# Routed attention and a tanh-shrink MLP on one core: the order of value products, narrow sum products, and some earlier steps

## The chip, the cores and the metric

The kernel runs on one core of a Trainium2 chip. The metric is the device time of one execution in microseconds (us), median of several runs. A difference of about 0.2% can be told from no change.

## The reference, cut to what matters

```python
# q, k, v: (4, 8, 768, 64); centroids: (8, 16, 64); w_in: (512, 2048); w_out: (2048, 512)
q_assign = argmax(q_n @ c_n.T)          # the nearest of 16 centroids, for each query
k_assign = argmax(k_n @ c_n.T)          # and for each key
scores = where(q_assign == k_assign, q @ k.T / 8, -1e9)
attn = softmax(scores)                  # over the 768 keys
x = (attn @ v), heads side by side      # (3072, 512)
h = x @ w_in
out = (h - tanh(h)) @ w_out             # (3072, 512)
```

All arithmetic is float32 in effect. The two weight matrices come in as 64-bit floats and are rounded on the chip.

## The kernel before, in words

**Order of the work.** The order on every engine is written out by hand: the builder runs through a Python loop over 96 `steps` (L856, L983) and each engine carries out its instructions in the order in which they were issued. Nothing is rescheduled later. A pair `n` is one batch element and two heads, so there are 16 pairs, four for each of the four batch elements; a pair has two halves of 384 queries, and each half has three steps of 256 keys. The first twelve steps are the first halves of pairs 0 to 3, the next twelve their second halves; from pair 4 on a pair's halves follow each other.

**A step.** `begin` (L411) computes the scores `sc` of the *following* step on TensorE and the exponential on ScalarE; `select` (L443) multiplies by the routing mask on VectorE: it compares a `row` of query codes with a key code (L451). `value` (L466) then multiplies the resulting weights `e` with the values into `av` (L473). In the first halves of pairs 1 to 3 (`masked`) the mask comes instead from a small extra product with one-hot codes `hot` (L430). The row sums that softmax divides by are products with a matrix of ones: for the first halves of pairs 0 to 3 (`summed`, L350) they are taken on TensorE in every step, four products of 64 columns (L482), of which two fit beside each other in the array; elsewhere GpSimd adds the weights up (L460, L464) and one product follows (L501). `take` (L489) copies `av` to `xT`; `total` (L494) copies the sums to `den`. For pairs that are not `soon` (L517; `soon` are pairs 2, 3, 7, 11 and 15) the sums travel through DRAM to be inverted: `list` (L511), `compact` (L520, back as `each`), `invert` (L526), `spread_out` (L532), `scale` (L539), one per step. The others are divided on the spot (`divide`, L543), and GpSimd adds their sums up in `wholes` (L507).

**Getting a pair ready** (`before`, L860) runs steps ahead in numbered stages: 0 `turns` transposes q and k on TensorE (`pt`, L300), ScalarE copies them out (`t`, L307), and the next loads are issued on SP; 1 `similar` (L313) multiplies with the centroids, four products of 32 columns that fit beside each other (`sim`, L319), copied by ScalarE (L324); 2 `route` (L326) transposes (`pr`, L332) and finds the codes on VectorE (L338 to L345); 3 `publish` (L359) writes the codes to DRAM (L364, L368, L370); for pairs 1 to 3 also 4 `spread_both` (L382: `hot`, read back over all partitions) and 5 `one_hot` (L390). In the loop, stage 1 comes first in its step (L1003), then `begin` (L1007), then `value` (L1013). Stage 0 is called between the pieces of other TensorE work (L1061); where a step has none, that is after the values and sums.

**The weights.** `fetch` (L185, GpSimd's queue) loads one of 32 pieces of 512 KB into one of three `raw` buffers, `rest_of` (L195) takes its low words on ScalarE (L140) and `round_piece` (L200) its high words on VectorE (L145 to L152) and fetches the piece after the next two. How many pieces belong to a step is written in `paces` (L980).

**The MLP** of batch element 0 is done plainly (L557) between the steps 12 to 47. Those of elements 1 to 3 use seven products of quarters instead of eight (`strassen_items`, L722): eight times seven `up_product` (`pu`, L761), then seven times three `down_product` (`pd`, L809). `right_factors` (L711) forms differences of `xT` on VectorE first; four of the seven up products need them, of the others the first two in order (`PRODUCTS`, L617: 1, 2, 6, 7, 4, 5, 3) do not. `up_product` puts the quarters of h together in `G` on VectorE (L747), and `shrink` (L749) subtracts the tanh: ScalarE takes the tanh of a tile of 768 columns (L751) and GpSimd subtracts it (L752). `fetch_factors` (L678) loads the factors of the item after the next into one of three `stream` buffers over SP's queue. The last element's items (L1072 to L1105) come after the loop; a check of all inputs and sums on VectorE (L1077 to L1098) stands after the first two of them.

PSUM holds two double tiles for scores and transposes, one tile for `av`, and three tiles for everything else (L164 to L166).

Of the kernel before, what the change touches and what calls it, by code (L numbers as in the profile page):

```python
# [30 lines left out]
F32 = mybir.dt.float32  # L31
# [3 lines left out]
ALU = mybir.AluOpType  # L35
ACT = mybir.ActivationFunctionType
AX = mybir.AxisListType

P = 128
# [18 lines left out]
def kernel(  # L58
# [43 lines left out]
    smallest = const.tile([P, 2 * len_pieces], F32, name="smallest")  # L102
    largest = const.tile([P, 4 * (HP - 1)], F32, name="largest")
    each = const.tile([P, 2 * (B * (HP - 1) - 1), 2 * TB // P], F32, name="each")
    flag = const.tile([1, 1], I32, name="flag")

    out_r = out.rearrange("(b p j) m -> b j p m", p=P, j=NCH)
# [46 lines left out]
    def fast():  # L154
# [195 lines left out]
        def summed(n: int, half: int):  # L350

            return n < HP and half == 0
# [113 lines left out]
        def value(n: int, half: int, s: int):  # L466
            e = weights.pop((n, half, s))
            if s == 0:
                avs[n, half] = ps_a.tile([P, TB], F32, name="av", tag="a")
            for i in range(2):  # L470
                j = 2 * s + i
                for h in range(2):
                    nc.tensor.matmul(  # L473
                        avs[n, half][h * D : h * D + D], lhsT=vals[n][:, h, j], rhs=e[i][:, h],
                        start=(j == 0), stop=(j == NCH - 1),
                    )
            if summed(n, half):
                if s == 0:
                    sums[n, half] = ps_f.tile([P, TB], F32, name="den", tag="f")
                for i in range(2):  # L480
                    for h in range(2):
                        nc.tensor.matmul(  # L482
                            sums[n, half][h * D : h * D + D], lhsT=ones, rhs=e[i][:, h],
                            start=(s + i == 0), stop=(2 * s + i == NCH - 1),
                        )

        dens = {}

# [5 lines left out]
        def total(n: int, half: int):  # L494

            s = sums.pop((n, half))
            ps = s
            if not summed(n, half):
                ps = ps_f.tile([P, TB], F32, name="den", tag="f")
                for h in range(2):  # L500
                    nc.tensor.matmul(  # L501
                        ps[h * D : h * D + D], lhsT=ones, rhs=s[:, h], start=True, stop=True
                    )
            t = dens[n, half] = sump.tile([P, TB], F32, name="den")
            nc.scalar.activation(out=t, in_=ps, func=ACT.Copy, bias=EPS)
            if soon(n):
                nc.gpsimd.tensor_tensor(out=wholes, in0=wholes, in1=t, op=ALU.add)  # L507
                return
            lists[n, half] = dram.tile([2, TB], F32, name="list")
            for h in range(2):  # L510
                nc.sync.dma_start(lists[n, half][h : h + 1], t[h * D : h * D + 1])  # L511

# [4 lines left out]
        def soon(n: int):  # L517
            return pairs[n][1] == HP - 1 or n == HP - 2

        def compact(n: int, half: int):  # L520
            spots[n, half] = each[:, len(spots)]
            nc.sync.dma_start(
                spots[n, half], lists.pop((n, half)).rearrange("h n -> (h n)").rearrange("(p i) -> p i", p=P)
            )

        def invert(n: int, half: int):  # L526
            t = spots[n, half]
            nc.vector.reciprocal(out=t, in_=t)
            back = lists[n, half] = dram.tile([2, TB], F32, name="back")
            nc.sync.dma_start(back.rearrange("h n -> (h n)").rearrange("(p i) -> p i", p=P), t)  # L530
# [177 lines left out]
            late_pools["G"] = late_pools["g"].tile([P, HF, 2, 2, TB], F32, name="G")  # L708
            late_pools["S1"] = late_pools["left"].tile([P, HF, TB], F32, name="S1")

        def right_factors(b: int):  # L711

            d = diffs[b] = late_pools["diff"].tile([P, 3, CH, TB], F32, name="diff")
            for c in range(CH):
                x, y = xT[b * HP + c], xT[b * HP + CH + c]
                for out, u, w in (
                    (d[:, 0, c], x[:, 1], x[:, 0]), (d[:, 1, c], y[:, 1], d[:, 0, c]),
                    (x[:, 1], y[:, 1], x[:, 1]), (d[:, 2, c], y[:, 0], d[:, 1, c]),
                ):
                    nc.vector.tensor_tensor(out=out, in0=u, in1=w, op=ALU.subtract)  # L720

        def strassen_items(b: int):  # L722
            base = (b - 1) * PER
# [4 lines left out]
            def up_product(i: int, k_: int, between):  # L728
                which = PRODUCTS[k_]
                x = [xT[b * HP + c] for c in range(CD)]  # L730
                d = diffs[b]
                right = {
                    1: [x[c][:, 0] for c in range(CH)], 2: [x[CH + c][:, 0] for c in range(CH)],
                    3: [x[CH + c][:, 1] for c in range(CH)], 4: [d[:, 2, c] for c in range(CH)],
                    5: [d[:, 0, c] for c in range(CH)], 6: [d[:, 1, c] for c in range(CH)],
                    7: [x[c][:, 1] for c in range(CH)],
                }[which]
                if k_ == 0:
                    held[i] = (
                        late_pools["s"].tile([P, TB], F32, name="s"),  # L740
                        late_pools["u"].tile([P, 2, TB], F32, name="u"),
                    )
                s, u = held[i]
                g = G[:, i]

                def add(out, x, y):
                    nc.vector.tensor_tensor(out=out, in0=x, in1=y, op=ALU.add)  # L747

                def shrink(f: int):  # L749
                    th = late_pools["th"].tile([P, 2, TB], F32, name="th")  # L750
                    nc.scalar.activation(out=th, in_=g[:, f], func=ACT.Tanh)  # L751
                    nc.gpsimd.tensor_tensor(  # L752
                        out=g[:, f].rearrange("p a n -> p (a n)"),
                        in0=g[:, f].rearrange("p a n -> p (a n)"),
                        in1=th.rearrange("p a n -> p (a n)"), op=ALU.subtract,
                    )

                ps = ps_f.tile([P, TB], F32, name="pu", tag="f")
                for c in range(CH):
                    for r in halves:  # L760
                        nc.tensor.matmul(  # L761
                            ps[r], lhsT=streams[base + i][:, c, k_, r], rhs=right[c],
                            start=(c == 0), stop=(c == CH - 1),
                        )
                if which == 1:
                    nc.scalar.copy(out=s, in_=ps)
                    fetch_factors(base + i + 2)
                elif which == 2:
                    add(g[:, 0, 0], ps, s)
                elif which == 6:  # L770
                    add(u[:, 0], ps, s)
                elif which == 7:
                    add(u[:, 1], ps, u[:, 0])
                elif which == 4:
                    add(g[:, 1, 0], ps, u[:, 1])
                elif which == 5:
                    add(u[:, 0], ps, u[:, 0])
                    add(g[:, 1, 1], ps, u[:, 1])
                    shrink(1)
                else:  # L780
                    add(g[:, 0, 1], ps, u[:, 0])
                    shrink(0)
                between()
                if k_ == len(PRODUCTS) - 1:

                    nc.gpsimd.tensor_tensor(out=left1[:, i], in0=g[:, 0, 1], in1=g[:, 1, 1], op=ALU.add)
                    nc.gpsimd.tensor_tensor(
                        out=g[:, 0, 1], in0=g[:, 0, 0], in1=g[:, 0, 1], op=ALU.subtract
                    )
                    streams.pop(base + i)  # L790
# [283 lines left out]
        for it in tail[:2]:  # L1074
            it[2](lambda: None)

# [213 lines left out]
```

## Time and profile before

| | us |
|---|---|
| median of three runs | 1012.71 (1012.15 to 1013.81) |
| the profiled execution, its own time | 1012.54 |
| its span, first to last instruction | 1010.8 |
| TensorE busy (PE) | 987.7 |
| VectorE busy (DVE) | 551.7 |
| GpSimd busy (POOL) | 502.8 |
| ScalarE busy (ACT) | 298.8 |

In views of the profile, PE is the matmul side of TensorE and PEld its weight loader, SP the engine that issues most transfers. A timeline line gives the start, the time from the first start to the last end of the merged instructions, engine, line, operation, output and inputs, the array's shape (rows*columns), the operand's shape and how many records were merged; in brackets the idle time before it and what ended it. A float32 matmul leaves two records and a transpose one. Records overlap, since matmuls are pipelined; how long a group holds TensorE is read from its start to the start of the next.

### The profile page before, as it was taken

To read this page: it belongs to the slowest core of one execution; us is meant where nothing else is said; L and a number is where in the kernel's file an instruction comes from. 1 tells how busy PE (TensorE), PEld (TensorE's weight loads), DVE (VectorE), ACT (ScalarE), POOL (GpSimd) and SP (SyncE) were. 2 spreads that over 40 slices of the span, in tenths; PEclk is the share of its full clock that TensorE was granted. 3 is DMA by queue.
4 is the path that set the end of the run, shared out by engine and by line. 5 is a ranking of instruction groups with operands and counts; after the bars stand their busy time and mean duration, and the time that the engine had idled before them with its cause. 6 is when DMAs were issued, how large, how long until landed. Compare 5 with 4: busy or idle time off the path is not lost.

```text
span 1010.8 us, 16557 instructions
## 1 busy us (share of the span) xinstructions
PE 987.7 (98%) x6444; PEld 470.6 (47%) x6444; DVE 551.7 (55%) x1047; ACT 298.8 (30%) x458; POOL 502.8 (50%) x343
## 2 busy tenths in 40 slices
PE   8989999999999999999999999999999999999997
PEld 4433443344443334444455555444445555444665
DVE  6457887737666566747544357655645336543011
ACT  4434443233432323332331222324331221122000
POOL 1014344545354554865777244675679345465600
PEclk9999999999999999999999999999999999999999
DMA  7653434214564823453445637344443232233221
GB/s 218 174 135 114 134 125 127 72 51 125 134 176 139 261 90 123 135 169 110 173 123 178 189 128 216 108 147 119 146 162 92 98 108 81 92 110 122 104 95 40
DMA packets 115681, 132.46 MB, mean 131 GB/s; under 512 B 62688, under 2 KB 95372, under 8 KB 112908
## 3 DMA queue, kind: packets, MB, share of 16 engines
q1 hardware_dynamic: 109212, 109.80, 35.7%
q0 software_dynamic: 6240, 21.50, 6.2%
q8 instruction: 53, 0.87, 0.4%
q14 instruction: 32, 0.26, 0.1%
q10 hardware_dynamic: 144, 0.03, 0.0%
HBM read 110.14 MB, written 21.17 MB: 130 GB/s over the span
## 4 chain that ended last, share of the span: by engine, by line
PE 91%; DVE 3%; DMA 1%; ACT 1%; POOL 1%; issue 1%; SPq 0%; DVEq 0%; ACTq 0%; POOLq 0%
PE pd L809 20%; PE pu L761 20%; PE sc L419 13%; PE av L473 13%; PE o L584 8%; PE h L568 8%; PE sim L319 2%; PE den L501 2%; PE pt L300 2%; PE den L482 1%; PE warm L270 1%; ACT t L307 1%; POOL G L752 1%; PE pr L332 1%; DMA hot<-q_codes 1%
## 5 line engine op out<-in xcount | busy, mean ns | idle before, releaser
L464 POOL TENSOR_TENSOR sum<-sum,e 128x768 f32<-128x768 f32 x112 | 207.3, 1850 | 106.5 <-DVE e L451 102.8
L451 DVE SCALAR_TENSOR_TENSOR e<-row,code,sc 128x384 f32<-128x384 bf16 x336 | 185.5, 608 | 94.7 <-ACT sc L441 78.6
L809 PE MATMUL pd<-stream,G 128*64 128x256 f32 x1728 | 192.4, 379 | 2.4 <-POOL G L752 2.4
L441 ACT ACTIVATE sc<-sc 128x768 f32<-128x768 f32 x168 | 126.2, 792 | 209.5 <-PE sc L419 207.4
L809 PEld LDWEIGHTS pd<-stream,G 128*64 128x64 f32 x1728 | 123.5, 137 | 70.5 <-issue 8.0
L473 PE MATMUL av<-e,vals 128*64 128x384 f32 x768 | 147.0, 502 | 4.7 <-ACT xT L492 3.8
L419 PE MATMUL sc<-t,t 64*128 64x384 f32 x768 | 149.9, 509 | 0.3 <-ACT e L441 0.3
L752 POOL TENSOR_TENSOR G<-G,th 128x768 f32<-128x768 f32 x48 | 87.4, 1833 | 104.6 <-ACT th L751 104.6
L761 PE MATMUL pu<-xT,stream 128*64 128x384 f32 x768 | 134.6, 487 | 0.7 <-DVE top L340 0.7
L761 PE MATMUL pu<-diff,stream 128*64 128x384 f32 x576 | 103.5, 488 | 1.9 <-DVE u L747 1.5
L419 PEld LDWEIGHTS sc<-t,t 64*128 64x128 f32 x768 | 66.0, 186 | 73.6 <-issue 41.6
L460 POOL TENSOR_TENSOR sum<-e 128x768 f32<-128x768 f32 x28 | 58.0, 2071 | 70.9 <-DVE e L451 62.6
L473 PEld LDWEIGHTS av<-e,vals 128*64 128x64 f32 x768 | 47.1, 136 | 89.6 <-issue 83.2
L761 PEld LDWEIGHTS pu<-xT,stream 128*64 128x64 f32 x768 | 54.6, 137 | 68.5 <-issue 61.5
L568 PE MATMUL h<-xT,w_in 128*64 128x384 f32 x512 | 86.2, 486 | 0.1
L584 PE MATMUL o<-w_out,g 128*64 128x512 f32 x384 | 86.1, 593 | 0.0
L751 ACT ACTIVATE th<-G 128x768 f32<-128x768 f32 x48 | 40.3, 843 | 123.0 <-DVE G L747 119.4
L761 PEld LDWEIGHTS pu<-diff,stream 128*64 128x64 f32 x576 | 40.5, 137 | 52.5 <-issue 44.3
L747 DVE TENSOR_TENSOR G<-pu,u 128x384 f32<-128x384 f32 x72 | 39.8, 553 | 40.8 <-PE pu L761 40.5
L568 PEld LDWEIGHTS h<-xT,w_in 128*64 128x64 f32 x512 | 36.6, 137 | 46.0 <-issue 44.7
L584 PEld LDWEIGHTS o<-w_out,g 128*64 128x64 f32 x384 | 27.3, 137 | 49.8 <-issue 49.3
L820 DVE TENSOR_TENSOR c<-pd,du 128x256 f32<-128x256 f32 x36 | 15.1, 420 | 62.8 <-PE pd L809 62.8
(121 smaller groups left out, 850.2 us busy)
## 6 DMA issues: line engine op xcount, KB each, us to landing
stream<-up_factors SPq DMA_DIRECT2D x24, 896.0 KB
stream<-down_factors SPq DMA_DIRECT2D x21, 1024.0 KB
raw<-in_moe_w_in_dram POOLq DMA_DIRECT2D x16, 512.0 KB, 5.3
raw<-in_moe_w_out_dram POOLq DMA_DIRECT2D x16, 512.0 KB, 4.4
again<-in_moe_w_in_dram SPq DMA_DIRECT2D x32, 256.0 KB
again<-in_moe_w_out_dram SPq DMA_DIRECT2D x32, 256.0 KB
x<-in_q_dram SPq DMA_DIRECT2D x32, 192.0 KB
x<-in_k_dram SPq DMA_DIRECT2D x32, 192.0 KB
```

The source lines that it names most:

```text
L419: nc.tensor.matmul(sc[i][:, h, 0:TB], lhsT=turned[n, 1][r].rearrange("p a n -> p (a n)")[:, j * P : (j + 1) * P], rhs=turned[n, 0][r, half ...
L441: nc.scalar.activation(out=out, in_=sc[i][:, :, 0:TB], func=ACT.Exp, scale=SCALE)
L451: nc.vector.scalar_tensor_tensor(out=e[:, h], in0=rows[n, half][:, h], scalar=codes[n][:, 1, j // HCH, h, j % HCH : j % HCH + 1], in1=sc[: ...
L460: nc.gpsimd.tensor_tensor(out=s, in0=pair[0], in1=pair[1], op=ALU.add)
L464: nc.gpsimd.tensor_tensor(out=s, in0=s, in1=pair[i], op=ALU.add)
L473: nc.tensor.matmul(avs[n, half][h * D : h * D + D], lhsT=vals[n][:, h, j], rhs=e[i][:, h], start=(j == 0), stop=(j == NCH - 1),)
L568: nc.tensor.matmul(h[r], lhsT=w_in[i][:, c, o * P : (o + 1) * P][:, r], rhs=xT[c][:, half], start=(c == 0), stop=(c == CD - 1),)
L584: nc.tensor.matmul(acc[sub][r], lhsT=gs[f % HF][:, f // HF, sub * P : (sub + 1) * P][:, r], rhs=w_out[f // FQ][:, f % FQ], start=(f == seq ...
L751: nc.scalar.activation(out=th, in_=g[:, f], func=ACT.Tanh)
L752: nc.gpsimd.tensor_tensor(out=g[:, f].rearrange("p a n -> p (a n)"), in0=g[:, f].rearrange("p a n -> p (a n)"), in1=th.rearrange("p a n -> ...
L761: nc.tensor.matmul(ps[r], lhsT=streams[base + i][:, c, k_, r], rhs=right[c], start=(c == 0), stop=(c == CH - 1),)
L809: nc.tensor.matmul(ps[r], lhsT=left(i)[:, r], rhs=t[:, i], start=(i == 0), stop=(i == HF - 1))
```

## The change

Six edits. (1) From pair 4 on, in the step that has stage 1, the step's values are issued before the similarities and the following scores. (2) In the summed steps the sums are split off (`sum_up`); for pairs 0 and 1 the four products have 32 columns each, one for each half of the keys and head, so that the sums come as two parts, which are added after the trip through DRAM (`other`). A stage 0 of that step is issued before the sums. (3) In the last of the eight up items `shrink` of the first quarter pair is done in two halves, the first as soon as product 2 is there. (4) `right_factors` works on half of the tiles at a time; from element 2 on the first half is issued one step earlier. (5) In the last element the first two products of item 1 come before the third of item 0, and everywhere `fetch_factors` is issued at the third product, not the first. (6) `paces` differ in steps 2, 4, 6, 8 and 9: 1, 0, 2, 1, 2 where it was 0, 2, 1, 2, 1.

```diff
             if summed(n, half):
-                if s == 0:
-                    sums[n, half] = ps_f.tile([P, TB], F32, name="den", tag="f")
-                for i in range(2):
-                    for h in range(2):
+                weights[n, half, s] = e
+
+        def sum_up(n: int, half: int, s: int):
+            e = weights.pop((n, half, s))
+            if s == 0:
+                sums[n, half] = ps_f.tile([P, TB], F32, name="den", tag="f")
+            for i in range(2):
+                for h in range(2):
+                    if soon(n):
                         nc.tensor.matmul(
                             sums[n, half][h * D : h * D + D], lhsT=ones, rhs=e[i][:, h],
                             start=(s + i == 0), stop=(2 * s + i == NCH - 1),
                         )
+                        continue
+
+                    r = h * D + i * D // 2
+                    nc.tensor.matmul(
+                        sums[n, half][r : r + D // 2], lhsT=ones[:, 0 : D // 2], rhs=e[i][:, h],
+                        start=(s == 0), stop=(s == NS - 1), tile_position=(0, r),
+                    )
...
-            nc.scalar.activation(out=t, in_=ps, func=ACT.Copy, bias=EPS)
+            parts = 2 if summed(n, half) and not soon(n) else 1
+            nc.scalar.activation(out=t, in_=ps, func=ACT.Copy, bias=EPS / parts)
...
-            lists[n, half] = dram.tile([2, TB], F32, name="list")
-            for h in range(2):
-                nc.sync.dma_start(lists[n, half][h : h + 1], t[h * D : h * D + 1])
+            lists[n, half] = dram.tile([parts, 2, TB], F32, name=f"list{parts}")
+            for i in range(parts):
+                for h in range(2):
+                    r = h * D + i * D // 2
+                    nc.sync.dma_start(lists[n, half][i, h : h + 1], t[r : r + 1])
...
+            t = lists.pop((n, half))
+            for i in range(t.shape[0]):
+                nc.sync.dma_start(
+                    other if i else spots[n, half],
+                    t[i].rearrange("h n -> (h n)").rearrange("(p i) -> p i", p=P),
+                )
...
+            if summed(n, half):
+                nc.vector.tensor_tensor(out=t, in0=t, in1=other, op=ALU.add)
             nc.vector.reciprocal(out=t, in_=t)
...
-        def right_factors(b: int):
+        def right_factors(b: int, c: int):
...
+            if c == 0:
+                diffs[b] = late_pools["diff"].tile([P, 3, CH, TB], F32, name="diff")
+            d = diffs[b]
+            x, y = xT[b * HP + c], xT[b * HP + CH + c]
...
+                def shrink(f: int, halves_=slice(0, 2)):
+                    t = g[:, f, halves_]
+                    th = late_pools["th"].tile([P, 2, TB], F32, name="th")[:, halves_]
+                    nc.scalar.activation(out=th, in_=t, func=ACT.Tanh)
...
                 if which == 1:
                     nc.scalar.copy(out=s, in_=ps)
-                    fetch_factors(base + i + 2)
                 elif which == 2:
                     add(g[:, 0, 0], ps, s)
+                    if i == HF - 1:
+                        shrink(0, slice(0, 1))
                 elif which == 6:
+                    fetch_factors(base + i + 2)
                     add(u[:, 0], ps, s)
...
                     add(g[:, 0, 1], ps, u[:, 0])
-                    shrink(0)
+
+                    shrink(0, slice(1 if i == HF - 1 else 0, 2))
...
-        paces = dict(enumerate((0, 0, 0, 2, 2, 0, 1, 2, 2, 1, 1, 0, 2, 2, 2, 2, 2, 2, 2, 3, 2)))
+        paces = dict(enumerate((0, 0, 1, 2, 0, 0, 2, 2, 1, 2, 1, 0, 2, 2, 2, 2, 2, 2, 2, 3, 2)))
...
+            values_first = 1 in stages and not summed(n, half)
+            if values_first:
+                value(n, half, s)
             if 1 in stages:
                 stages[1]()
...
-            value(n, half, s)
+            if not values_first:
+                value(n, half, s)
+            if summed(n, half):
+                if 0 in stages:
+                    stages.pop(0)()
+                sum_up(n, half, s)
...
             if "raw" in late_pools:
                 todo += [check_done, check_done, check_on, check_on]
+                if p == HP - 1 and half == 1 and s == NS - 2:
+                    todo += [lambda b=b, c=c: right_factors(b, c) for c in range(CH - 1)]
...
             if at in fills and "raw" in late_pools:
-                right_factors(b - 1)
+                for c in range(CH - 1 if at > 4 * HALF else 0, CH):
+                    right_factors(b - 1, c)
...
-        right_factors(B - 1)
+        right_factors(B - 1, CH - 1)
         tail = strassen_items(B - 1)
+
+        PRS = len(PRODUCTS)
+        tail = tail[:2] + tail[PRS : PRS + 2] + tail[2:PRS] + tail[PRS + 2 :]
```

More of the change, by code (lines that the diff above doesn't have):

```diff
@@ L104 @@
     each = const.tile([P, 2 * (B * (HP - 1) - 1), 2 * TB // P], F32, name="each")
+    other = const.tile([P, 2 * TB // P], F32, name="other")
     flag = const.tile([1, 1], I32, name="flag")
@@ L521, in compact @@
             spots[n, half] = each[:, len(spots)]
-            nc.sync.dma_start(
-                spots[n, half], lists.pop((n, half)).rearrange("h n -> (h n)").rearrange("(p i) -> p i", p=P)
-            )
+            t = lists.pop((n, half))
[4 more added lines that the diff above has]
+                )
         def invert(n: int, half: int):
             t = spots[n, half]
+            if summed(n, half):
+                nc.vector.tensor_tensor(out=t, in0=t, in1=other, op=ALU.add)
             nc.vector.reciprocal(out=t, in_=t)
@@ L709, in open_late @@
             late_pools["S1"] = late_pools["left"].tile([P, HF, TB], F32, name="S1")
-        def right_factors(b: int):
[L713 to L720, printed above, removed]
+        def right_factors(b: int, c: int):
[3 more added lines that the diff above has]
+            x, y = xT[b * HP + c], xT[b * HP + CH + c]
+            for out, u, w in (
+                (d[:, 0, c], x[:, 1], x[:, 0]), (d[:, 1, c], y[:, 1], d[:, 0, c]),
+                (x[:, 1], y[:, 1], x[:, 1]), (d[:, 2, c], y[:, 0], d[:, 1, c]),
+            ):
+                nc.vector.tensor_tensor(out=out, in0=u, in1=w, op=ALU.subtract)
         def strassen_items(b: int):
@@ L747, in add @@
                     nc.vector.tensor_tensor(out=out, in0=x, in1=y, op=ALU.add)
[L749 to L756, printed above, removed]
+                def shrink(f: int, halves_=slice(0, 2)):
+                    t = g[:, f, halves_]
+                    th = late_pools["th"].tile([P, 2, TB], F32, name="th")[:, halves_]
+                    nc.scalar.activation(out=th, in_=t, func=ACT.Tanh)
+                    t, th = (x.rearrange("p a n -> p (a n)") for x in (t, th))
+                    nc.gpsimd.tensor_tensor(out=t, in0=t, in1=th, op=ALU.subtract)
                 ps = ps_f.tile([P, TB], F32, name="pu", tag="f")
```

## The prediction

> **What bounds the kernel now.** First the page: busy time, the span in slices, the chain's shares.
>
> ```profile
> PE 987.7 (98%) x6444; PEld 470.6 (47%) x6444; DVE 551.7 (55%) x1047; ACT 298.8 (30%) x458; POOL 502.8 (50%) x343
> PE   8989999999999999999999999999999999999997
> PE 91%; DVE 3%; DMA 1%; ACT 1%; POOL 1%; issue 1%; SPq 0%; DVEq 0%; ACTq 0%; POOLq 0%
> ```
>
> TensorE bounds it: 98% busy, 91% of the chain. Only the first slices show holes. A gain must shorten what TensorE does or fill one of its gaps. So next I read its timeline around each place the edits touch. A stage 1 from pair 4 on:
>
> ```profile
> 257.04 1.53 PE L300 MATMUL pt<-ident,x 128*128 128x128 f32 x12
> 258.81 1.54 PE L319 MATMUL sim<-t,bd 128*32 128x384 f32 x8 [0.23 <-ACT t L307]
> 260.28 1.56 PE L419 MATMUL sc<-t,t 64*128 64x384 f32 x8
> 261.77 1.51 PE L473 MATMUL av<-e,vals 128*64 128x384 f32 x8
> ```
>
> and one where a weight product stands between transposes and similarities:
>
> ```profile
> 503.45 1.53 PE L300 MATMUL pt<-ident,x 128*128 128x128 f32 x12
> 504.91 1.51 PE L761 MATMUL pu<-diff,stream 128*64 128x384 f32 x8
> 506.35 0.85 PE L319 MATMUL sim<-t,bd 128*32 128x384 f32 x8
> 507.13 1.56 PE L419 MATMUL sc<-t,t 64*128 64x384 f32 x8
> ```
>
> From start to start `sim` holds TensorE 1.47 us in the first, 0.78 in the second. In the first its operands have just been copied: it waits 0.23 for ACT, and its records start in two groups 0.70 apart, as ACT's second copy lands; in the second all start within 0.02. So a gated place loses 0.31 (`pt` 1.77 against 1.46) and 0.69, mostly unseen as idle.
>
> The summed steps, where the page shows the early holes, on TensorE and on ACT:
>
> ```profile
> 65.58 1.56 PE L419 MATMUL sc<-t,t 64*128 64x384 f32 x8
> 68.49 0.50 PE L430 MATMUL sc<-hot 64*128 64x384 bf16 x4 [1.35 <-DVE hot L398]
> ...
> 77.36 2.55 PE L473 MATMUL av<-e,vals 128*64 128x384 f32 x8 [3.83 <-ACT xT L492]
> 79.70 2.16 PE L482 MATMUL den<-e,ones 128*64 128x384 f32 x8
> ```
>
> ```profile
> 76.27 0.67 ACT L140 ACTIVATE rest<-raw 128x512 uint32<-128x512 uint32 x1 [4.56 <-DMA raw<-in_moe_w_in_dram]
> 76.84 0.46 ACT L492 COPY xT<-av 128x384 f32<-128x384 f32 x1
> ```
>
> The 3.83 is put down to `take` (L492), but that copy stands behind a `rest` that waited 4.56 for a weight piece. The stretch 77 to 92 then shows a clock of 0.89: `av` there takes 2.34 and `den` 2.09 from start to start, against 1.34 and 1.39.
>
> The last element:
>
> ```profile
> 848.20 0.87 PE L501 MATMUL den<-sum,ones 128*64 128x384 f32 x4 [0.91 <-POOL sum L464]
> 859.55 0.87 PE L761 MATMUL pu<-diff,stream 128*64 128x384 f32 x4 [0.36 <-DVE diff L720]
> 864.52 1.51 PE L761 MATMUL pu<-diff,stream 128*64 128x384 f32 x8 [1.52 <-DVE u L747]
> ```
>
> ```profile
> 930.71 3.19 PE L809 MATMUL pd<-stream,G 128*64 128x256 f32 x28
> 935.32 4.97 PE L809 MATMUL pd<-stream,G 128*64 128x256 f32 x44 [1.41 <-POOL G L752]
> ```
>
> **The skill.** "TensorEngine Tiling (Array Packing)", Tiling Modes: 128x32 gives four tiles, 128x64 two, and changing the mode drains TensorE. The trace agrees: four `sim` products of 32 columns take 0.78 together, four `den` products of 64 take 1.39; `sc` before a product of its own mode takes 1.39, before `av` 1.49, so a change costs about 0.10. "TensorE: Matmul & The Clock Gate", Part 1: idle gaps over about 3.4 us throttle the clock. The trace agrees: 3.83 idle, then 0.89. The same page, Architectural detail: ScalarE and VectorE are strictly first in, first out. Agrees: `take` at 76.84 behind the `rest`.
>
> **The change, part by part,** against the profiled execution (1012.54; span 1010.8; median 1012.71).
>
> *A. Values first, 12 places.* Ahead of `sim` now stands `av`, 1.34 long, which covers the 0.23 and the second copy. Before, seven places are gated: five (258.8, 302, 346, 389, 565) lose 0.31 + 0.69, two (448, 684) 0.60 in `sim` alone; five are not (152.6, 216, 506, 626, 742). No stage 1 of before has this order, so its mode changes are bounded: none more than before (0), or one more at each of the 12 places (1.2 in all); I take 0.10 at each of the seven gated ones. Gain 5 x 0.90 + 2 x 0.60 + 5 x 0 = **5.7** (5.2 to 6.4). `av` comes 2.3 (ungated) to 3.3 earlier; its select had ended 5.6 to 10.3 ahead of it at these places, so 2.4 or more is left. The next scores, and so the exponential and select behind them, come later by at most 1.34; the least margin of the steps after is 2.28.
>
> *B. Sums of 32 columns, and paces.* Six steps (0 to 5) have four such products: 0.70 + 0.08 + 0.10 of mode change = 0.88 instead of 1.39, 0.5 each. That four overlap here as in `sim` is an assumption (bounds 0.70 to 1.40). Up to the codes of pair 3: step 0 1.06 (also `pt`'s wait for its load at 27.4 is rearranged), steps 1, 2, 4, 5 0.5 each, step 3 1.3 (`den` now lies between `pt` and a gated `sim`): 4.3. On VectorE, `qc` of pair 3 waits behind rounding pieces (code ready 54.17, `qc` 57.94); with pace 0 in step 4 they are gone and it follows at about 52.4 (its transpose `pq` at 56.28 - 4.3 = 52.0, 0.28 long, and the way to VectorE), 5.5 earlier. From `qc` to the end of `one_hot` is 68.43 - 57.94 = 10.5 (`q_codes` 2.82, `hot` 5.93, issues, two comparisons), so `hot` is there at 62.9; TensorE arrives 4.3 earlier than the 66.97 at which it began to wait, 62.65. Of the 1.35 some 0.25 stays, and L430 starts 5.6 earlier.
> The 3.83: its cause was that the fetch of this piece waited behind `one_hot` on VectorE; pieces now come in other steps, and one `rest` instead of two stands ahead of `take`. I keep 1.7 of new small waits in steps 9 to 12 (`rest` of 0.67 behind an exponential, at 0.4, 0.8, 0.5). Gain 3.8 - 1.7 = 2.1, and the slow clock's 1.0 + 0.7 = 1.7 goes with the gap. Sum 5.6 + 2.1 + 1.7 = **9.4** (7 to 11.5: with none of the small waits 1.7 more, with more of them or a later `qc`, 2.4 less).
> The cost side: SP issues six more DMAs (`list`, `each`/`other`; the widest SP issue shown is 0.61), and `x(4)`'s loads now stand ahead of `each`; the divisions are needed many steps later. The `each + other` addition is some 0.1 on VectorE: nothing.
>
> *C. Halved tanh.* Before, the down products of the first quarter pair wait for a whole tanh (0.84) and subtraction (1.82) after the last up product: 0.75 lost at 511 and at 747, 1.57 at 931.7 (idle 1.41 plus the broken pipe). One half is now done three products (2.6 each) ahead, the other takes half the time. Gain **3.1** (2.3 to 3.1).
>
> *D. The last element.* `den` L501 waits for a sum of GpSimd (idle 0.91, 1.08 from start to start): GpSimd comes late from the subtractions, and the halved ones of C let it start sooner; 0 to 1.08, I take all. `pu` at 859.55 loses 0.53, since its difference is made only then; the first half moves one step ahead. At 864.5 it loses 1.69: its tile comes free late, because `u` stood behind eight differences (8 x 0.55) and 3.2 us of checks; four go earlier and four plain products (1 and 2 of two items) now stand before the first difference product. Gain **3.3** (1.5 to 3.3). Streams are fetched about 2.6 later; they land 4.4 after the issue and the least slack to use is 13.4: nothing.
>
> Sum: 5.7 + 9.4 + 3.1 + 3.3 = 21.5. The profiled execution becomes 991.0; the median lies 0.17 above: **991.2**.
>
> **The rivals.**
> *R1, a new wait in the first 80 us.* `other` and `each` stand on SP behind `x(4)`, and the addition on VectorE waits for them, with pair 3's codes queued behind it. For: VectorE is strictly in order. Against: before, the last of these loads ends at 51.36, so if that stays, `each` lands at about 53.7 and `qc` at 54.0, 1.6 late; a hole then stays before L430 and, with `rest` as before, the 2.1 and the clock's 1.7 are not won: 991.2 + 1.6 + 2.1 + 1.7 = 996.6.
> *R2, the change doesn't do what it says:* the four 32-column sums run one after the other or two by two, 0.5 x 6 lost: 994.2.
> *R3, slower.* One mechanism: at the 12 places `av` now stands ahead of the following scores, so that TensorE, in order, waits for VectorE's select there. It decides from selects about 6.5 us later than before: the margins left are 2.4 to 8.0, mean about 4.7, and 21.5 of gain over 12 places is 1.8 each. At 7 us late each place waits 2.3: 28 lost, 1019. For: VectorE carries the differences and the rounding too. Against: selects in this stretch follow the exponential within a step, no edit adds VectorE work from step 12 on, and the least margin of any place is positive.
>
> **How the numbers follow.** Forecast 0.76; R1 0.15, R2 0.06, R3 0.03. Low end: B at 11.5 (2.1 less), A at 6.4 (0.7 less), and the early waits of `pq` and `pr` that the waits view has (1.0 and 0.6) gone as well: 991.2 - 4.4 = 986.8. High end: R1's 996.6 and D at its 1.5 instead of 3.3, 998.4. Outside stay R3 and mishaps that add up, some 2 in 10. A measurement of this kernel can tell about 0.2% from no change (2 us): faster 0.95 (forecast, R1, R2, less a little), same 0.02, slower 0.03.
>
> **What would show it.** A: at the 12 places `sim` 0.78 from start to start, no wait for `t`, and none of `av` for a select. B: `den` in steps 0 to 5 at 0.78 to 0.88; no wait of `sc` for `hot` over 0.5; no clock under 1 in 60 to 90; step 12's `av` (92.04 before) at about 82.6. C: no wait of `pd` for `G` over 0.3. D: no wait of `pu` for `u`. A `sim` still in two groups, a gap over 3 us in 50 to 90, or a wait of `av` for `e` would make it wrong.

## The result, and the profile after

| | before | after |
|---|---|---|
| median, us | 1012.43 | 995.62 |
| ratio | 1 | 0.9834 (95% interval 0.9817 to 0.9851) |
| the profiled execution: time, span | 1012.54, 1010.8 | 994.73, 993.0 |
| TensorE busy | 987.7 | 977.2 |

The change saves 16.8 us in the medians and 17.8 in the two spans, where 21.5 were forecast. The time lies inside the range, 4.4 above the forecast, near where the rival R1 would have ended, though not by what R1 said. The page after:

```profile
PE 977.2 (98%) x6444; PEld 466.5 (47%) x6444; DVE 555.2 (56%) x1049; ACT 299.4 (30%) x461; POOL 500.2 (50%) x346
PE   8998999999999999999999999999999999999997
PE 92%; DMA 3%; DVE 3%; SPq 1%; issue 1%; ACT 0%; DVEq 0%
```

TensorE is as full as before, with less to do. It was also "busy" while its operands were late (products of 1.47 us that take 0.78), which is a part of the 10.5 by which its busy time fell.

To place the gain, take the n-th value product of both kernels (their number is the same) and subtract the start times. This shift is constant wherever nothing differs, and steps where something does. (A row named by a step is read at the first value product of that step.)

| from | shift, us | what lies between |
|---|---|---|
| step 0 | -0.60 | the warm-up products at the start (L270, now L271) took 5.62 in this execution, 6.44 in that of before |
| step 6 | -4.10 | narrow sums, transposes ahead of sums |
| step 10 | -10.79 | no waits for `hot` and for `rest` any more |
| step 12 | -5.83 | **a new wait** |
| step 13 | -6.11 | |
| step 95 | -12.88 | seven steps of stage 1, 0.84 x 5 + 0.60 x 2 = 5.40; twice a halved tanh, 0.69 each |
| first down product of element 3 | -16.34 | the boundary of the last element, 3.46 |
| the next | -17.97 | the third halved tanh, 1.63 |

A step of stage 1 after, in TensorE's timeline (it answers to the one at 257.04 before):

```profile
250.94 1.53 PE L301 MATMUL pt<-ident,x 128*128 128x128 f32 x12
252.40 1.51 PE L474 MATMUL av<-e,vals 128*64 128x384 f32 x8
253.84 0.85 PE L320 MATMUL sim<-t,bd 128*32 128x384 f32 x8
254.62 1.56 PE L420 MATMUL sc<-t,t 64*128 64x384 f32 x8
```

From start to start: `pt` 1.46 (1.77 before), `sim` 0.78 (1.47), `av` 1.44 (1.34): the values cover both copies, at 0.10 for a change of mode. No `av` waits for a select there.

The early steps on TensorE:

```profile
28.27 0.85 PE L495 MATMUL den<-e,ones 128*32 128x384 f32 x8
...
68.26 1.51 PE L474 MATMUL av<-e,vals 128*64 128x384 f32 x8 [0.34 <-ACT xT L505]
...
76.34 1.62 PE L420 MATMUL sc<-t,t 64*128 64x384 f32 x8 [0.73 <-ACT e L442]
...
83.35 2.93 PE L420 MATMUL sc<-t,t 64*128 64x384 f32 x8 [2.66 <-DVE e L452]
86.21 1.51 PE L474 MATMUL av<-e,vals 128*64 128x384 f32 x8
```

The narrow sums hold TensorE 0.67 to 0.79. The waits of 1.35 and 3.83 are gone. But the scores of step 13 wait 2.66 for the first select (L452), since the tile of scores comes free only then; and they then take 2.86 instead of 1.49. The windows view of 83.3 to 86.2 (after the two times: busy time and instructions of PE, PEld, DVE, ACT and POOL, then the granted clock, the DMA share and GB/s) says why: half the clock.

```profile
83.30:86.20 2.90, 2.85 (x8) 1.22 (x8) 2.90 (x5) 0.80 (x1) 1.92 (x2) 0.50 0.67 192
```

VectorE ahead of that select:

```profile
59.59 0.31 DVE L399 TENSOR_SCALAR hot<-hot,mine_code 128x384 bf16<-128x384 bf16 x1
63.33 0.56 DVE L562 TENSOR_TENSOR xT<-xT,den 128x384 f32<-128x384 f32 x1 [3.42 <-DMA den<-back]
64.87 0.17 DVE L548 TENSOR_TENSOR each<-each,other 128x6 f32<-128x6 f32 x1 [0.98 <-DMA other<-list]
...
68.92 1.66 DVE L146 TENSOR_SCALAR w_in<-raw 128x512 uint32<-128x512 uint32 x1
...
82.07 2.18 DVE L452 SCALAR_TENSOR_TENSOR e<-row,code,sc 128x384 f32<-128x384 bf16 x4
```

It stands idle for 3.42 and 0.98 us, for two transfers of sums, with two weight pieces queued behind; from 64.87 to the select it works without a pause. TensorE, which had waited for others until now, has caught up with VectorE.

### The profile page after: what moved, and what is told of

The parts are those of the page before. It is cut to its first block, busy times and chain, and to the rows that moved or that the text cites. A ratio compares the mean times of both kernels' runs of the same rounds, so it can differ in the third digit from the quotient of the medians.

```text
span 993.0 us, 16579 instructions
## 1 busy us (share of the span) xinstructions
PE 977.2 (98%) x6444; PEld 466.5 (47%) x6444; DVE 555.2 (56%) x1049; ACT 299.4 (30%) x461; POOL 500.2 (50%) x346
## 4 chain that ended last, share of the span: by engine, by line
PE 92%; DMA 3%; DVE 3%; SPq 1%; issue 1%; ACT 0%; DVEq 0%
PE pd L832 22%; PE pu L781 21%; PE sc L420 13%; PE av L474 12%; PE o L605 8%; PE h L589 8%; PE pt L301 2%; PE den L514 2%; PE sim L320 1%; DMA x<-in_k_dram 1%; DMA hot<-q_codes 1%; PE warm L271 1%; PE pr L333 1%; DVE e L452 1%; DMA q_codes<-qc 1%
## 5 line engine op out<-in xcount | busy, mean ns | idle before, releaser
L452 DVE SCALAR_TENSOR_TENSOR e<-row,code,sc 128x384 f32<-128x384 bf16 x336 | 185.3, 607 | 92.6 <-ACT sc L442 71.4
L776 POOL TENSOR_TENSOR G<-G,th 128x768 f32<-128x768 f32 (+1 forms) x51 | 88.1, 1738 | 98.7 <-ACT th L774 98.7
L774 ACT ACTIVATE th<-G 128x768 f32<-128x768 f32 (+1 forms) x51 | 40.9, 806 | 117.6 <-DVE G L769 114.0
```

Source lines behind the costliest of these rows:

```text
L452: nc.vector.scalar_tensor_tensor(out=e[:, h], in0=rows[n, half][:, h], scalar=codes[n][:, 1, j // HCH, h, j % HCH : j % HCH + 1], in1=sc[: ...
L774: nc.scalar.activation(out=th, in_=t, func=ACT.Tanh)
L776: nc.gpsimd.tensor_tensor(out=t, in0=t, in1=th, op=ALU.subtract)
```

## The theory and its rivals

**Theory:** the four parts do what the forecast said, except that the early gain is capped by VectorE's queue: idle behind the sums' transfers, then six pieces and a division, then the select. **Rivals:** the new paces themselves made the wait; the narrow sums with their second transfer did; or the amount of rounding is what counts, not the idle time.

## The experiments

**1. Values first, alone, on the kernel before.**

```diff
-            if 1 in stages:
+            values_first = 1 in stages and not summed(n, half)
+            if values_first:
+                value(n, half, s)
+            if 1 in stages:
                 stages[1]()
...
-            value(n, half, s)
+            if not values_first:
+                value(n, half, s)
```

> The kernel before with the first edit alone: in the steps from pair 4 on that have stage 1, the values go ahead of the similarities. The two traces put this edit's part at 5 x 0.84 + 2 x 0.60 = 5.4 us, at the seven places where the similarities waited for the copies of the transposes, and at 0 at the other five. If the edit is independent of the rest, the time is 1012.4 - 5.4 = 1007.0 and the shift of the value products against the kernel before grows by 0.84 or 0.60 at the same seven steps. Rival: in the changed kernel a part of it comes from the other edits (selects that are earlier for them); alone, the values then wait for their selects and the gain is below 4, 1008.5 or more.

1006.60, ratio 0.9945 (0.9928 to 0.9961). The shift against the kernel before grows by 0.84 or 0.85 at five steps, by 0.60 at two, and by nothing at the others: 5.40, the same as in the whole change. The edit is independent of the rest, and the rival falls.

**2. Sums of 64 columns in the changed kernel.**

```diff
-                    if soon(n):
+                    if True:
                         nc.tensor.matmul(
...
-            parts = 2 if summed(n, half) and not soon(n) else 1
+            parts = 1
...
-            if summed(n, half):
-                nc.vector.tensor_tensor(out=t, in0=t, in1=other, op=ALU.add)
```

> The changed kernel with the sums of pairs 0 and 1 in four products of 64 columns again (one part, no second transfer, no addition), in the new order and with the new paces. Theory: the 0.5 us that each of the six steps saves on TensorE is given back, because step 12 is set by VectorE, whose queue there starts from the sums of pair 1 (the addition at 64.87 waits for the transfer of the second part); 3 us more on TensorE ahead of step 6 and a shorter trip of the sums nearly cancel: 995.6, between 994.5 and 997, and the wait of the scores for the select shrinks from 2.66. Rival: the 3 us carry through to the end, 998.6.

995.96, ratio 0.9837 (0.9819 to 0.9854): no difference from the changed kernel that can be told. The shift at step 6 is -2.03 instead of -4.10, at step 13 -5.31 instead of -6.11. The time is the theory's; its sentence on the wait was wrong, for that stays at 2.67. VectorE's line tells why:

```profile
65.83 0.19 DVE L546 RECIPROCAL each<-each 128x6 f32<-128x6 f32 x1 [3.77 <-DMA each<-list]
```

With narrow sums TensorE gets the sums of pair 1 done 2.1 us earlier, and their longer trip in two parts takes 1.1 of that: VectorE goes on at 64.87 instead of 65.83. Only this 1.0 reaches the select (0.80: 82.07 against 82.87). The narrow sums are thus no cause of the wait, and hardly of the gain.

**3. The paces of before in the changed kernel.**

```diff
-        paces = dict(enumerate((0, 0, 1, 2, 0, 0, 2, 2, 1, 2, 1, 0, 2, 2, 2, 2, 2, 2, 2, 3, 2)))
+        paces = dict(enumerate((0, 0, 0, 2, 2, 0, 1, 2, 2, 1, 1, 0, 2, 2, 2, 2, 2, 2, 2, 3, 2)))
```

> The changed kernel with the weight paces of the kernel before. Theory: the new paces are needed; with the old ones the codes of pair 3 stand behind rounding again, and TensorE waits for the one-hot codes or for a rest behind a late weight piece: 2 to 6 us more, 998 to 1001. Rival: the new paces have themselves made the wait of 2.66 us (two pieces in step 9 instead of one), and with the old ones it is shorter: 995.6 or less.

998.46, ratio 0.9858 (0.9839 to 0.9876), 2.8 above the change in the medians. Both old waits are back:

```profile
66.08 0.50 PE L431 MATMUL sc<-hot 64*128 64x384 bf16 x4 [2.68 <-DVE hot L399]
...
75.98 1.87 PE L474 MATMUL av<-e,vals 128*64 128x384 f32 x8 [3.16 <-ACT xT L505]
```

The wait for `hot` is 2.68, where it was 1.35: TensorE comes to it 3.7 earlier than in the kernel before, the codes only 2.4. The shift at step 13 is only -1.43 in this execution, while the kernel of experiment 1, which has none of these edits, stands at -1.56 there. So the narrow sums and the new order win little without the paces, which clear the way for the codes. (By the medians this kernel gains 14.1 on the one before; less the 11.9 of the other three parts, about 2 are left.) The new paces are not the cause of the wait at 83.35 but what makes it the last one left: with the old ones as many pieces, six, stand behind the sums, and VectorE comes to the first select only at 86.75.

**4. Rounding ahead of the sums in step 7.**

```diff
-            todo += late + later.pop(at, [])
+            sums_back = late + later.pop(at, [])
...
+            if at != 7:
+                todo += sums_back
...
+            if at == 7:
+                todo += sums_back
```

> The changed kernel with one queue order changed on VectorE: in step 7 the two pieces of rounding stand ahead of the scaling of pair 0 and the inversion of pair 1, which wait for transfers of sums (3.42 and 0.98 us idle at 60 to 64.9). Theory: the wait of 2.66 us of the scores for the first select (and the slow clock behind it, 1.37) comes from these idle 4.4 us, because VectorE is never idle from 64.87 to that select; with rounding in them the select ends 2 to 4 us earlier, the wait falls below 1 us, and the time is 992.6 (991.5 to 993.6). Rival: the pieces cannot be rounded in that gap since their fetches land only at 63.2, or the later inversion puts the same wait elsewhere; then nothing is won, 995.6 within 0.7.

992.00, ratio 0.9794 (0.9777 to 0.9810): faster than the changed kernel, whose interval it doesn't touch. Three lines of VectorE and one of TensorE:

```profile
64.57 0.55 DVE L562 TENSOR_TENSOR xT<-xT,den 128x384 f32<-128x384 f32 x1
...
67.89 0.99 DVE L548 TENSOR_TENSOR each<-each,other 128x6 f32<-128x6 f32 x1 [2.77 <-DMA other<-list]
...
80.94 2.18 DVE L452 SCALAR_TENSOR_TENSOR e<-row,code,sc 128x384 f32<-128x384 bf16 x4
```

```profile
82.22 1.97 PE L420 MATMUL sc<-t,t 64*128 64x384 f32 x8 [1.66 <-DVE e L452]
```

The gap is filled with two pieces, and the scaling follows them with no wait (the addition after it still waits 2.77); the select comes 1.1 earlier though this execution reached step 1 1.1 later than that of the change, so 2.3 in all. The idle time of VectorE between `hot` and the select is not gone: it falls by 1.4, from 4.4 to 3.0. Another 0.45 is no idle time. An addition of GpSimd (L521), beside which VectorE is slow, falls on a rounding in the change (L146: 1.66 instead of 0.42) and on the short addition here (L548: 0.99 instead of 0.17). The wait of the scores falls to 1.66, not below 1 as expected, and the clock stays at 1.00. Counted from step 1, this trace is 3.2 better at step 12: 0.4 and 0.9 at steps 9 and 11, where two smaller waits are gone, 1.0 from the shorter wait and 1.0 from the scores behind it. That the order of VectorE's queue in step 7 set the select is shown; idle time is the larger part of it, and a part of the wait is something else.

**5. One piece of step 10 in step 13.**

```diff
-        paces = dict(enumerate((0, 0, 1, 2, 0, 0, 2, 2, 1, 2, 1, 0, 2, 2, 2, 2, 2, 2, 2, 3, 2)))
+        paces = dict(enumerate((0, 0, 1, 2, 0, 0, 2, 2, 1, 2, 0, 0, 2, 3, 2, 2, 2, 2, 2, 3, 2)))
```

> The changed kernel with one weight piece rounded in step 13 instead of step 10. Theory: the first select of step 12 is set by the amount of work that is queued on VectorE ahead of it, with no idle time from 64.87 on; one piece (1.9 us of VectorE) less ahead of it brings it 1.9 earlier, the wait of 2.66 falls to 0.8 and the half clock behind it goes (1.4): 3 us, 992.6. Rival: VectorE has only been late because it follows ScalarE and TensorE, or the third piece of step 13 delays a select there: 995 or more.

995.86, ratio 0.9839 (0.9823 to 0.9856): nothing won, as the rival said. Yet at step 12 it is 3.2 us better: against the change the shift goes from +1.85 (a later start) to -1.36, and the wait for the select is 0.95. Then it goes back to +0.50 before step 15:

```profile
112.57 1.83 PE L589 MATMUL h<-xT,w_in 128*64 128x384 f32 x10 [1.63 <-DVE g L596]
```

So the amount of rounding counts as well, and the theory had the size right for step 12. But it had not asked where the third piece of step 13 goes.

**6 to 8. The other edits.** Three kernels undo one edit each in the changed one:

```diff
-                    if i == HF - 1:
-                        shrink(0, slice(0, 1))
...
-                    shrink(0, slice(1 if i == HF - 1 else 0, 2))
+                    shrink(0)
```

> The changed kernel with the last tanh of each of the three elements whole again. The two traces put this edit at 0.69 + 0.69 + 1.63 = 3.0 us (the shift grows by that at the first down products of each element): 998.6. Rival: the halved subtractions also let GpSimd be in time for the sums at the end of the loop, so that the 1.08 there comes back too: 999.7.

998.45, ratio 0.9862 (0.9844 to 0.9881). The shift against the change grows by 0.69, 0.70 and 1.63 at the first down products, 3.0; the sums at the end of the loop are not late. The rival falls.

```diff
-                if p == HP - 1 and half == 1 and s == NS - 2:
-                    todo += [lambda b=b, c=c: right_factors(b, c) for c in range(CH - 1)]
...
-        right_factors(B - 1, CH - 1)
+        for c in range(CH):
+            right_factors(B - 1, c)
```

> The changed kernel with all eight differences of an element formed after its last step, as before, and the new order of the last element's products kept. Theory: the two edits of the last element do the same work twice: four products without differences take 5.2 us of TensorE, eight differences 4.4 us of VectorE, so that at most the wait for the difference of 0.5 comes back; 995.6 to 996.1. Rival: the additions of u still stand behind eight differences and the checks (4.4 + 3.2 us), and 1.7 us or more comes back: 997.3 or more.

997.98, ratio 0.9861 (0.9843 to 0.9878). The time lies in the rival's range, but half of it comes by another way. Of the shift, 2.16 is lost at the last element: about 1.1 at a wait for the sums (idle 0.91), the rest behind eight differences and the checks. The first part is a surprise. GpSimd's timeline of this kernel, then that of the change:

```profile
832.17 0.56 POOL L849 DMA_DIRECT2D out_dram<-c  x1 [4.37 <-DVE c L843]
832.75 3.92 POOL L465 TENSOR_TENSOR sum<-sum,e 128x768 f32<-128x768 f32 x2
```

```profile
826.73 3.71 POOL L465 TENSOR_TENSOR sum<-sum,e 128x768 f32<-128x768 f32 x2 [0.34 <-DVE e L452]
830.76 0.56 POOL L849 DMA_DIRECT2D out_dram<-c  x1 [0.32 <-DVE c L843]
```

The last two additions of the loop were late because the issue of an output transfer, which waits for `c`, stood ahead of them in GpSimd's queue. Adding items to the step's list, which is cut into equal parts between the products, moved the last two selects, and with them the additions, ahead of it.

```diff
-        tail = tail[:2] + tail[PRS : PRS + 2] + tail[2:PRS] + tail[PRS + 2 :]
```

> The changed kernel with the last element's products in the old order, the early differences kept. Theory: the checks of 3.2 us on VectorE stand between the second product and the additions of u, so the wait of TensorE for u comes back, shortened by the four differences that are done earlier (2.2): 0 to 1.7 back, 996.4. Rival: the early differences alone have removed the waits, 995.6.

996.03, ratio 0.9841 (0.9825 to 0.9857). In the trace 0.65 is lost, with a wait for `u` of 0.42, inside what was expected; the medians can't tell it. Of the 3.46 of this boundary, 2.16 need the early differences (1.1 of them through GpSimd's queue), 0.65 the new order of products, and 0.65, by subtraction, come with either. The later fetch of the factors was undone in no kernel; no wait for `stream` is seen in the change.

**9 to 12. Can the rest of the wait be removed?** The changed kernel was run again beside the first two of these.

> The changed kernel unaltered, on the same chip as the two above, for their difference: 995.6 within 1; either theory expects its profile to show the scores of step 13 waiting for the select of step 12 by 2 to 2.7 us.

996.30, ratio 0.9839 (0.9825 to 0.9852). Its profile shows less than expected: it waits 1.66 for the select, and 1.48 for an exponential a step earlier, and the clock does not fall. But this execution took 993.39, and the other four of this run 995.98 to 996.51 with a lower mean clock (0.997 to 0.998 against 1.000): the profile shows the untypical one. The shift at step 13 is -7.29 in it, where the first profile of the change had -6.11.

On top of experiment 4, a piece goes from step 10 to step 11:

```diff
-        paces = dict(enumerate((0, 0, 1, 2, 0, 0, 2, 2, 1, 2, 1, 0, 2, 2, 2, 2, 2, 2, 2, 3, 2)))
+        paces = dict(enumerate((0, 0, 1, 2, 0, 0, 2, 2, 1, 2, 0, 1, 2, 2, 2, 2, 2, 2, 2, 3, 2)))
```

> Rounding first in step 7 as in the run of that name, and one weight piece moved from step 10 to step 11, where it stands behind the selects of step 12. Theory: the two take different parts of VectorE's queue ahead of the first select (idle 4.4 us, and 1.9 us of work), so that the wait that was left, 1.66 and 0.4 behind it, goes; unlike step 13, step 11 has slack on VectorE: 992.0 - 2.0 = 990.0. Rival: what is left is TensorE's own work and ScalarE's exponentials, or the piece is missing later as it was when it was put in step 13 (1.85 lost there): 991.5 or more.

992.73, ratio 0.9802 (0.9788 to 0.9815): not better than experiment 4. The wait for the select is gone, and step 12 is 1.87 ahead. Before step 15 all of it is given back. TensorE and ScalarE there:

```profile
109.96 0.54 PE L589 MATMUL h<-xT,w_in 128*64 128x384 f32 x2 [1.57 <-DVE g L596]
```

```profile
107.88 0.67 ACT L141 ACTIVATE rest<-raw 128x512 uint32<-128x512 uint32 x1 [3.88 <-DMA raw<-in_moe_w_out_dram]
108.46 0.46 ACT L505 COPY xT<-av 128x384 f32<-128x384 f32 x1
108.82 0.88 ACT L594 ACTIVATE th<-h 128x384 f32<-128x384 f32 x2
```

It is what the kernel before showed at 76: a `rest` waits for its weight piece, with `take` and the tanh behind it. The next two kernels go after one cause each.

On top of the last, pair 1 is inverted in step 8, behind the rounding:

```diff
+                        i += (n, half) == (1, 0) and i > 1
...
-            if at != 7:
+            if at not in (7, 8):
```

> The run before, and the inversion of pair 1 with what follows it one step later, behind the rounding of step 8, so that VectorE no longer stands idle for the second part of the sums (2.77 us). Theory: with the wait for the select gone this idle time costs nothing any more: the same as the run before within 0.7. Rival: the select is still the last, and 1 us more is won.

993.32, ratio 0.9807 (0.9794 to 0.9820). The medians can't tell it from the run before, as expected. In its trace (the slowest of the five executions, 994.83) that idle time is gone and step 12 is 0.2 earlier for it, but the later trip costs more: the products of h then wait 2.6 for the scaled values of pair 1.

And on top of the last but one, a piece goes from step 14 to step 16:

```diff
-        paces = dict(enumerate((0, 0, 1, 2, 0, 0, 2, 2, 1, 2, 0, 1, 2, 2, 2, 2, 2, 2, 2, 3, 2)))
+        paces = dict(enumerate((0, 0, 1, 2, 0, 0, 2, 2, 1, 2, 0, 1, 2, 2, 1, 2, 3, 2, 2, 3, 2)))
```

> The run with rounding first and a piece moved from step 10 to 11, and besides one of the two pieces of step 14 moved to step 16. There the second rest of step 14 waited 3.88 us for its weight piece (landed at 107.9), with the copy of the values and the tanh of h behind it on ScalarE, and TensorE lost 1.57 us for g. Theory: the wait that was taken away at step 12 has only come back at the next place where ScalarE is held by a late weight piece; with that piece out of the way it stays away: 992.7 - 1.8 = 990.9. Rival: the supply of weight pieces bounds this whole stretch, and the wait shows at step 15 or 16 instead: 992.7 within 0.7.

994.26, ratio 0.9814 (0.9801 to 0.9828). The rival holds as to the place, while the time is 0.9 above its range. Step 15 is 1.8 ahead, as the theory had it, and before step 18 more than that, 2.9, is lost, with the same sign on ScalarE and a wait of TensorE behind it:

```profile
139.97 0.66 ACT L141 ACTIVATE rest<-raw 128x512 uint32<-128x512 uint32 x1 [5.02 <-DMA raw<-in_moe_w_out_dram]
```

```profile
142.03 2.80 PE L589 MATMUL h<-xT,w_in 128*64 128x384 f32 x16 [2.86 <-DVE g L596]
```

Four kernels (experiment 5 and these three) took the wait for the select away, or most of it, and found a wait again within a few steps, three of them behind the same kind of `rest`. A piece is fetched when VectorE has rounded one three pieces back, so pieces put off come late together. That their supply bounds the stretch from step 12 to 18 for any paces was not tried; experiment 4, at 992.0, is the best that was found.

## Why the prediction was right or wrong

| part | forecast | measured |
|---|---|---|
| A, values first | 5.7 | 5.40 |
| B, narrow sums and paces | 9.4 | 6.11 |
| C, halved tanh | 3.1 | 3.0 |
| D, the last element | 3.3 | 3.46 |
| sum | 21.5 | 18.0 |

The measured column is from one pair of profiled executions. B may hold up to 0.60 of the earlier start, and against the second profile of the change it is 7.3; in the medians the sum is 16.8, which leaves 4.9 for B if the other three are as measured.

**A** was right in place and mechanism: five gated steps, two half-gated, five at nothing. The five gave 0.84 each, not 0.90. The sum has a slip: it means to charge 0.10 for the mode at all seven places and charges it at five, so that it should have been 5.5. At the other two the gain was the full 0.60; there a product of the same 128x64 shape as `av` already stood ahead of `sim`. The margins held. **R3** did not come at its 12 places, but its mechanism came elsewhere: at step 12 TensorE stood behind a select.

**B** is the step that failed, and in one term: "I keep 1.7 of new small waits in steps 9 to 12". These came to 5.0. Up to step 10 B went as forecast: 11.1 without the small waits, and the shift was -10.79 there (up to 0.60 of it from the start). Then 0.86 was lost at step 11 and 4.10 at step 12. The 4.10 are the 2.66 and what the half clock adds to the scores (2.86 - 1.49 = 1.37). The forecast followed TensorE and ScalarE through these steps and let VectorE end its queue whenever TensorE needed it. It had the numbers for that: before, the first select started at 88.18, after a pause of only 0.87, so that with TensorE nearly 10 us earlier VectorE had to become late:

```profile
88.18 2.19 DVE L451 SCALAR_TENSOR_TENSOR e<-row,code,sc 128x384 f32<-128x384 bf16 x4 [0.87 <-ACT sc L441]
```

It priced the addition of the two parts at "nothing" and set the transfers aside, since "the divisions are needed many steps later". What is needed soon is what stands behind them in VectorE's order: experiment 4 shows it, by 3.6 us in the medians. Why some of the wait remains there stays open.

Its split of B was wrong too. The narrow sums were given 0.5 a step; experiment 2 shows that taking them away costs 0.3 in the medians. The paces carry this part (experiment 3), and of the narrow sums' gain on TensorE only the earlier end of the sums' trip arrives.
The codes of pair 3 went as forecast: `qc` started at 52.76 (52.4 forecast) and L431 waited no more. **R1** named the right instruction, the addition that waits for `other`, but put its harm on the codes, where it was 0.3 us; it did harm 12 us later, at the second pair. **R2** falls: four products of 32 columns do run together. That the time lies inside the range is in part luck: the range reaches so far up because of R1's wait, and a different wait filled it.

**C** was right to 0.1, in the size of each of its three places.

**D** was right in the sum, and wrong on one cause. The 1.08 at `den` was put down to GpSimd being late from whole subtractions; with these back (experiment 6) it stays away, and it returns when the differences are late (experiment 7), through the place of an output transfer in GpSimd's queue. The cover that four plain products give was overrated: alone, they leave a wait for `G` of 0.8.

## What to carry to other kernels

When a change lets the bound engine run ahead by many microseconds, work out when every other in-order engine reaches its next result for it, pauses included: the gain ends at the first that has no slack. An instruction that is needed much later may still be urgent to place well, if it waits for a transfer and other work stands behind it. And a piece of work that is moved out of one wait has to be followed to its new place, since it often makes the same wait there.

## What the runs showed of the hardware

- The length of a gap alone does not tell whether TensorE's clock falls. The Trainium skill, "TensorE: Matmul & The Clock Gate", Part 1, gives gaps over about 3.4 us as those to avoid; here the clock fell to 0.50 after 2.66 us (the change), 2.67 (experiment 2) and even 1.80 (the second kernel of experiments 6 to 8, 1.8 us after the products had begun again), while 2.86 (the last kernel of experiments 9 to 12) and 1.66 (experiment 4) left it at 1.00. The measurement decides. In the ten falls that the traces have between start and end of the work, the half clock lasted 3.41 us each time.
- A rounding instruction of VectorE (L146) takes 0.42 us alone and 1.66 where GpSimd adds two tiles (68.92 to 70.58, GpSimd at 69.26 to 70.28), 1.22 in another such place. "GPSIMD Engine Reference" of the Trainium skill (the table of properties) says that GpSimd shares its SBUF interfaces with VectorE; this trace agrees, at 0.8 to 1.2 us a time. In experiment 4 the addition of GpSimd comes at 67.86 to 68.86, and the rounding behind it takes 0.39.
- The profiled executions reach the first value product at 23.45 to 24.76, to within 0.02 in the order of the time that the warm-up products at the start took (5.6 to 7.2 us). In the kernels that share the changed opening, step 1 then starts between 30.0 and 31.8, since half of the transposes of step 0 come 0.66 to 1.42 late; in six of these eleven the profile names the landing of a load. A part of this is absorbed by the first wait that follows.
